# A gated-deltanet and MLP kernel on one core: half-chunk solves in one 64-row product, key loads on one queue, a new order list

## The chip, the cores and the metric

The kernel runs on one core of a Trainium2 chip. The metric is the device time of one execution in microseconds; the kernel before takes 277.19 us (median of three runs, 276.89 to 277.89). The profile is of one further execution, with a span of 275.1 us from the first to the last instruction. PE is TensorE, DVE is VectorE, ACT is ScalarE, POOL is GpSimd, and SP is SyncE, which here only issues DMA transfers.

## The reference

Two stages follow each other: a recurrence over 768 time steps for 4 batches of 8 heads with 48 features, and a two-layer MLP with a softplus between (3072 tokens, 384 to 2048 to 384).

```python
k_n = k / (norm(k) + 1e-6)
for t in range(S):                                   # S = 768
    readout = q[t] @ state                           # state: 48 x 48 per head
    y[t] = g[t] * readout
    v_old = state.T @ k_n[t]
    state = state + beta[t] * outer(k_n[t], v[t] - v_old)
x = y.transpose(0, 2, 1, 3).reshape(3072, 384)
out = softplus(x @ w_in) @ w_out
```

The readout at step t uses the state before step t. Inputs and outputs are float32; the kernel works in float16 with float32 accumulation.

## The kernel before

**Chunks.** The 768 steps are cut into 12 chunks of 64. Within a chunk the recurrence becomes a triangular system: with A the strictly lower part of the keys' products (scaled by beta and the norms), the corrected values u solve (1 + A) u = w, where w is v less what the state already holds for the keys. So each chunk needs the inverse of a 64 x 64 unit triangular block for each of 32 (batch, head) pairs. Two batches share the 128 partitions as 2 x 64 time steps; `HALF[r]` names those two ranges of 64, `QUAD[i]` the four ranges of 32, so `QUAD[2r]` is the first half of a chunk and `QUAD[2r + 1]` the second. The heads are split by m in two sets of eight, so most products come twice.

**Inverses.** Two neighbouring chunks are inverted together. The 32 x 32 diagonal blocks are inverted by column steps. For most pairs this is done as 16 x 16 blocks in 15 steps (`inverse`, L706; each step is one multiplication at L746 and one addition at L753), joined to 32 x 32 by the products `xmm` (L820) and `tmm` (L847). The steps run on VectorE for chunks 0 and 1, on GpSimd for the others. For chunks 8 and 9 (`LANES`) the 32 x 32 blocks are inverted directly in 31 steps on GpSimd (`wide_inverse`, L642; L679 and L685). Ahead of the steps stand the evicted key products, a transpose `ln` on VectorE (L713, L648) and the scales `bl` from beta and the norms (`lane_beta`, L394). After them come transposes on VectorE (L770, L779, L696) and casts on ScalarE (L800, L807, L701) to the tile `td`.

**Half blocks.** `halves` (L869) prepares, from the inverted diagonal blocks `td` and the keys' cross block, a tile `z`: its second-half rows are a copy of `td` made by an identity product (L879), its first-half rows the product of the cross block with `td` (L882).

**The chain of a chunk** (`chain`, L930): products of keys with the state, `ks` (L951); w on VectorE (L995, or L964 for chunk 0), after v was scaled by the norms at L973; `umm` (L1006), the diagonal blocks times w; a copy u1 to SBUF; `qs` (L951), queries with the state; `zu` (L1043), which adds the cross term to the second half; a copy u2; `smm` (L1076), the state's update, added on VectorE (L1093, state `s`); `ymm` (L1106), the outputs; the product with g (L1128); and a transpose into `xt`, by TensorE (L1147) for chunks 0 to 3 and 11, else by DMA.

**The MLP** (`dense`, L1178) takes the chunks in pairs, the first two and the last two singly: groups of up to six matmuls into `h` (L1194), the softplus on ScalarE (L1208), and groups of four matmuls into `o` (L1224), a copy and two stores. It has 96 groups of each of the two kinds.

**Loads.** k, q, v and g of a chunk come as two transfers of 192 KB each (`load`, L260). The rings of buffers are short: three for k, v and g, two for q. A load waits on its issuing engine until its buffer is free, and everything behind it waits too. Nearly all loads are issued by SyncE; `BY_ACT` (L121) names those that ScalarE issues. The weights are loaded by GpSimd in eight quarters, each held until a named load has landed.

**Order.** The program adds some 1137 items to a `Plan`, each with an engine, a cost, dependencies and buffers. A list written out at the end of the file, `_TABLE`, then says in which order they are issued: P112 is item 112 on TensorE, D on VectorE, A on ScalarE, G on GpSimd, S on SyncE. `follow` (L71) walks the list, hands out buffers and issues the instructions. It reads neither costs nor priorities: those serve whoever made the list. Each engine executes its items in the list's order, and an item that waits holds all that stand behind it on its engine.

Of the kernel before, what the change touches and what calls it, by code (L numbers as in the profile page):

```python
# [93 lines left out]
def kernel(  # L94
# [11 lines left out]
    nc = tc.nc  # L106
    B, H, S, D = q.shape
# [13 lines left out]
    BY_ACT = (("k", 0), ("k", 2))  # L121
# [31 lines left out]
    ident = pool.tile([P, P], F16, name="ident")  # L153
# [91 lines left out]
    HALF = [slice(0, 64), slice(64, 128)]  # L245
# [3 lines left out]
    def hd(ap):  # L249
        return ap[:, : H * D].rearrange("p (h d) -> p h d", h=H)  # L250
# [391 lines left out]
    def wide_inverse(cs, kk, kk_it, bl, bl_it, prio, prio2):  # L642
# [46 lines left out]
        for j in range(31):  # L689
            prev = add(  # L690
                "POOL", "step", 0.52 + 3.2e-3 * (31 - j) * (j + 1), lambda j=j: step(j),
                deps=[prev], bufs=[nn, tt, tmp], prio=prio,
            )
# [12 lines left out]
    def inverse(cs, kk, kk_it, bl, bl_it, on_dve, clear, prio, prio2, apart=0):  # L706
# [53 lines left out]
        for j in range(15):  # L760
            prev = add(
                en, "step", (0.42 if on_dve else 2 * fix) + 4 * per * (15 - j) * (j + 1), lambda j=j: step(j),
                deps=[prev], bufs=[nn, tt, tmp], prio=prio,
            )
# [165 lines left out]
    def chain(c, pr):  # L930
# [71 lines left out]
        def umm(m):  # L1002
            for pi in range(H):
                u = 16 * cl + 2 * pi + m
                for qd in range(4):
                    nc.tensor.matmul(  # L1006
                        hd(up[m].ap)[QUAD[qd], pi],
                        td.ap[QUAD[qd], u, :],
                        w1[m].ap[QUAD[qd], pi],
                        start=(pi == 0),  # L1010
                        stop=False,
                        skip_group_check=True,
                    )
# [3 lines left out]
                "PE", "umm", 0.22, lambda m=m: umm(m), deps=[a2[m], td_it],  # L1017
                bufs=[td, w1[m], up[m], u1[m]], prio=pr, mm=32, mode="3232",
# [21 lines left out]
        def zu(m):  # L1040
            for pi in range(H):
                for r in range(2):
                    nc.tensor.matmul(  # L1043
                        hd(up[m].ap)[QUAD[2 * r + 1], pi],
                        z.ap[QUAD[2 * r], 16 * cl + 2 * pi + m, :],
                        u1[m].ap[QUAD[2 * r], pi],
                        start=False,
                        stop=(pi == H - 1),
                        skip_group_check=True,
                    )  # L1050
# [4 lines left out]
                bufs=[z, u1[m], up[m], u2[m]], prio=pr, order=[c0], mm=16, mode="3232",  # L1055
# [246 lines left out]
S1 S0 A3 D111 P112 A2 D104 P105 G134 D135 A114 D107 A113 G132 S8 D133 A106 P115 P108 S6 D110 S9  # L1302
D118 S7 D109 A5 A4 S17 A136 A204 P205 D137 D138 A116 A117 D139 D140 D141 D142 D143 D144 D145 D146
D147 D148 D149 D150 D151 D152 D153 D154 D155 D156 P119 D157 D158 G97 A206 A207 P208 A197 G96 S10
S11 G227 G98 D159 P198 A199 A200 P201 A203 S18 A160 P162 A161 A190 S16 D125 D163 G103 A202 D169
P164 A165 S19 S20 D210 A209 D168 D228 S23 P166 D167 G99 P170 A172 D232 P174 A121 D120 P122 A189
D123 P171 D173 P175 P191 A177 G225 D176 D124 D226 A192 P126 D127 P183 S13 S12 D184 P181 D182 P178
A229 S39 S38 D230 P187 S22 A266 S21 D447 D128 D179 S14 S15 D211 A275 P276 S37 G267 P268 D269 D180
G100 A278 A188 P185 A186 P811 D231 S28 S29 A812 P212 A270 A214 P193 D277 P799 P279 D559 A194 P560
P813 D562 P195 G297 D281 D561 D213 P564 P129 D280 D298 A566 A196 P567 P569 A571 P563 D131 D130  # L1310
P577 D565 P568 S31 S30 D218 P219 S32 S33 D578 A814 D570 G102 P575 A299 A220 D221 P572 P222 D300
A800 D573 S47 P801 A802 D576 D574 S46 D224 P579 A580 G233 G234 S55 D223 P803 D271 S54 S36 S25 G235
G236 G237 A804 G238 G101 G239 G240 P581 G241 G242 G243 G244 D582 G245 G246 G247 G248 G249 P215
D216 G286 P287 P272 D273 P282 G250 G251 D252 D283 A289 P827 A288 D284 P805 A274 A828 S62 A254 A806
A346 P293 P809 D295 S24 P290 D291 G301 S45 S50 P256 S44 P829 A830 S60 P257 D253 A810 D294 D302
A258 S61 D217 D292 D285 D303 P837 S51 D296 D304 A368 D369 G607 P807 A808 P584 S63 P815 A255 G583
D586 D585 G357 G305 A838 P831 G306 G307 G308 P816 S27 P259 P817 P818 A832 P260 P839 A261 P262 P347
D349 A819 S49 A348 P264 D265 P835 P821 D263 S48 S35 G309 G310 S81 A836 G311 P588 D590 G312 G313
G314 P587 A589 A840 P591 P592 G315 G316 G317 S26 D652 P822 P593 P841 A595 P601 A370 D594 P599 P596
P823 D598 D597 P833 P608 P824 D602 A834 D600 D610 P612 P615 D371 G318 G319 A825 D609 A614 P603  # L1320
G320 G321 A604 S820 P617 G322 G323 P611 P605 D606 P843 A842 G342 A613 P616 A619 D618 P343 P620
P625 D324 P623 P844 A441 S34 A344 A326 D626 S80 S71 D624 P629 P627 P845 A338 S70 G417 A345 D628
P418 A419 D630 D622 P358 A420 A360 P865 A866 D359 G372 P328 D442 P855 A856 P361 D325 D363 S43 D362
P879 A880 P863 D621 P861 P329 P339 A327 D330 D340 P364 P332 A862 S85 S52 D365 S40 D373 D366 P885
G376 D367 D374 S41 A341 A864 A886 P859 A860 S84 P846 A847 S53 A439 P873 A874 D440 A496 P632 G631
S826 D633 P331 D634 P877 P869 A870 P353 D355 P350 P849 A333 D351 P334 A335 P636 P867 A868 S42 S69
A878 P850 P851 S90 P635 A637 D352 D354 D356 D375 P871 A872 G443 P639 P336 P640 D642 A638 P641 P857
A643 P644 D646 D645 A858 P883 A884 S78 S848 S59 P852 A853 P875 D409 P653 D654 P887 D655 S79 A337
P881 P410 D444 G377 G378 G379 G380 G381 G382 G383 G384 P656 P649 D412 D411 S68 A518 G428 P647 G385
D650 S56 D648 G386 G387 G388 G389 G390 P429 P657 P660 A876 A658 G391 A659 A882 G392 G393 P661 D445  # L1330
P662 P888 A664 P670 P889 P890 S76 D430 D431 D671 D519 A663 G394 S64 P668 S77 D669 P665 D666 A891
P421 P893 P894 P895 P896 S65 S651 D395 D422 A413 P414 D667 D423 A397 A416 A415 S854 P424 P399 P400
A897 D425 D396 A398 P435 S57 D436 A401 D426 S672 P917 D427 D437 P899 P900 P901 A918 P902 S892 A903
P432 D434 P941 A942 S91 D433 P905 P906 P915 A916 P919 A920 P674 P911 D438 P403 D446 A912 P402 P937
G520 D521 D673 D675 P907 A404 P939 A938 D676 S58 P405 D522 S898 A940 P908 P935 D523 P678 A936 P677
P927 S75 P925 G507 P508 A406 P681 A679 A680 S72 P683 A928 D509 A926 P929 P933 A510 D909 P682 A930
A684 D685 P407 P691 P689 D690 D692 A934 P913 P686 P497 D498 D687 D688 P921 G694 A914 D408 P931
S904 P943 S910 S67 A922 P695 G448 D697 P923 A492 P493 A932 P699 D696 P698 D499 S66 A924 D524 P944
P945 P946 A488 P489 A494 A495 P702 A700 P703 A701 S83 P704 A947 D490 S86 A706 G449 G450 G451 S693
S73 S948 P949 P712 G452 D705 G453 G454 G455 G456 G457 S82 P710 G458 G459 D713 G460 G461 G462 G463  # L1340
G464 G465 G466 G467 P950 P951 P952 G468 D711 A953 D491 P503 D504 D505 S714 P511 D513 D512 G469
G470 P955 G471 G472 G473 P956 P957 G474 G475 G476 G477 P958 G478 G479 G480 A959 P707 D708 D709
P500 D502 D501 P969 A970 S960 S89 P977 A978 P961 P514 P716 P971 A972 P989 D506 A990 P962 P979 A980
D515 P981 P991 A982 D516 D517 D525 S88 G481 A992 D482 P973 A974 P967 A968 P983 A984 A483 P963 P964
A965 S954 P985 A986 S87 D715 D718 P993 P484 A994 D717 P720 P719 P723 A485 D721 P987 D722 A988 P997
A998 P724 P486 S74 P725 P999 P975 D736 A727 D726 P728 D729 A976 G526 G527 G528 G529 G530 G531 G532
G533 G534 G535 G536 G537 G538 G539 P995 G540 D730 P733 D734 A996 G541 P731 G542 P737 G543 P1000
P1001 G544 G757 D732 D739 P1002 A1003 D738 P740 D742 S92 S93 S966 P741 P744 P1005 P1006 P1007
S1004 D546 A743 A487 P745 D747 P746 D748 P1008 A548 A1009 P752 P749 P754 P1011 P1012 D545 A547
P1013 P1014 D755 S735 D753 A1015 S756 P550 P549 A551 P1017 P1018 P1019 P1049 P1035 P552 A1050  # L1350
A1036 S1016 P553 P1027 A1028 P1023 A1024 P1020 S1010 D751 P1051 A1052 P1025 D750 P758 D760 D759
P1045 A1026 P1041 D554 A1046 A1042 P1031 A1032 P1039 A1040 P555 P761 P762 D764 P1043 A556 P765
P767 A763 P766 A1044 D1021 S1022 A769 P1033 A1034 P1037 A1038 S94 D768 P770 D771 D772 P1053 P1029
G778 A1030 P779 P775 S95 P773 D776 D780 P1047 P1055 P1056 D774 S777 A1054 P1057 D781 A1048 P1058
# [36 lines left out]
```

## Time and profile before

| What | Value |
|---|---|
| time, median of three | 277.19 us |
| span of the profiled run | 275.1 us, mean granted clock 0.969 |
| TensorE busy | 226.1 us |
| dense matmuls L1194 and L1224 | 77.2 and 71.3 us, 384 each |
| softplus on ScalarE, L1208 | 56.7 us, 96 |
| GpSimd 31 long steps, L679 and L685 | 16.7 and 17.1 us |
| GpSimd 60 short steps, L746 and L753 | 22.0 and 23.1 us |
| `umm`, L1006 | 9.7 us, 768 matmuls |
| `zu`, L1043 | 8.7 us, 384 matmuls |
| DMA moved | 29.07 MB, mean 106 GB/s |
| loads of k, q, v, g | median 4.7 to 6.0 us from issue to landing |

In the profile, busy time is the time in which an engine has an instruction in flight. Matmuls are pipelined, and a matmul that waits inside a group can count as busy, so a full row of TensorE doesn't mean that it works at its peak. The slices cut the span into 40 parts of 6.9 us, each digit being a share in tenths. Idle time of an engine is listed with what ended it. Item numbers of the order list don't appear in the profile: there an instruction is known by its line and its tiles.

### The profile page before, as it was taken

What the parts mean: (1) busy time and instruction counts of PE and PEld (TensorE: products, weight loads), DVE (VectorE), ACT (ScalarE), POOL (GpSimd) and SP (SyncE); (2) the same over time, 40 slices, a digit from 0 to 9 for tenths busy, and PEclk for the clock granted to TensorE, in tenths of its full rate; (3) what the DMA queues carried; (4) which work ended last, traced back from release to release, by engine and by line L of the source; (5) the groups of instructions that cost most, each with busy time, mean ns of one, the idle gap of its engine ahead of it and who ended that gap; (6) DMA issues with size and microseconds to landing.
All of it is one profiled execution on the core that took longest, in us unless ns stands there. A gap on an engine that the chain in (4) does not pass through costs nothing.

```text
span 275.1 us, 13296 instructions
## 1 busy us (share of the span) xinstructions
PE 226.1 (82%) x6030; PEld 150.5 (55%) x6030; DVE 165.7 (60%) x318; ACT 134.8 (49%) x230; POOL 141.1 (51%) x247
## 2 busy tenths in 40 slices
PE   0540357969898879999999999997599999999986
PEld 0430246757666555555665666553356655668754
DVE  6498589588996626896779956691757123412000
ACT  2241635433764357967447567154536356235620
POOL 8660023888917885287844788888887000000000
PEclk9999999995999979999999999999599999999999
DMA  8999999999998948455993146653312303400312
GB/s 109 144 174 193 173 164 156 181 175 150 142 160 140 135 75 169 84 104 97 151 150 61 33 90 122 116 115 59 64 27 62 76 17 63 84 14 20 71 46 61
DMA packets 113304, 29.07 MB, mean 106 GB/s; under 512 B 106464, under 2 KB 113248, under 8 KB 113248
## 3 DMA queue, kind: packets, MB, share of 16 engines
q1 hardware_dynamic: 105120, 24.19, 53.6%
q0 software_dynamic: 3968, 3.25, 7.6%
q10 hardware_dynamic: 4160, 0.79, 2.4%
q8 instruction: 47, 0.77, 1.2%
q14 instruction: 9, 0.07, 0.1%
HBM read 25.26 MB, written 4.72 MB: 109 GB/s over the span
## 4 chain that ended last, share of the span: by engine, by line
PE 39%; POOL 23%; DVE 11%; DMA 8%; issue 7%; SPq 6%; ACT 3%; DVEq 0%; POOLq 0%; ACTq 0%
PE o L1224 13%; PE h L1194 13%; SPq L268 6%; POOL t L685 6%; POOL tmp L679 6%; DMA qf<-in_q_dram 6%; POOL tt L753 4%; POOL tmp L746 4%; DVE kkm L599 3%; DMA gf<-in_g_dram 2%; PE d L1006 2%; PE d L1043 1%; DVE ln L713 1%; PE d L951 1%; PE d L882 1%
## 5 line engine op out<-in xcount | busy, mean ns | idle before, releaser
L1194 PE MATMUL h<-xt,w_in 128*128 128x512 f16 (+1 forms) x384 | 77.2, 338 | 0.9 <-ACT xt L236 0.6
L1208 ACT ACTIVATE ga<-h 128x512 f16<-128x512 f32 x96 | 56.7, 598 | 40.6 <-PE h L1194 39.3
L1224 PE MATMUL o<-w_out,ga 128*128 128x384 f16 x384 | 71.3, 329 | 1.3 <-DVE osb L238 0.7
L1224 PEld LDWEIGHTS <-ga 128*128 128x128 f16 x384 | 35.8, 98 | 24.4 <-issue 1.9
L1194 PEld LDWEIGHTS <-w_in 128*128 128x128 f16 x384 | 35.6, 101 | 22.6 <-issue 3.3
L433 PE MATMUL d<-ident,kn 128*128 128x128 f16 x96 | 9.4, 258 | 19.6 <-ACT kn L236 10.0
L753 POOL TENSOR_TENSOR tt<-tt,tmp 128x30 f32<-128x30 f32 (+7 forms) x60 | 23.1, 385 | 4.7
L746 POOL TENSOR_TENSOR tmp<-nn,tt 128x30 f32<-128x30 f32 (+7 forms) x60 | 22.0, 367 | 4.5
L236 ACT ACTIVATE u<-d 128x384 f16<-128x384 f32 x28 | 13.3, 492 | 21.8 <-PE d L1043 10.9
L236 ACT ACTIVATE kqx<-d 128x512 f16<-128x512 f16 x27 | 15.0, 593 | 16.2 <-PE d L433 13.4
L599 DVE TENSOR_TENSOR kkm<-d,both 128x512 f16<-128x512 f32 x32 | 20.5, 676 | 2.1 <-PE d L589 2.1
L236 ACT ACTIVATE osb<-o 128x384 f32<-128x384 f32 x19 | 9.3, 489 | 25.2 <-PE o L1224 23.1
L995 DVE TENSOR_TENSOR w<-vf,d 128x384 f16<-128x384 f32 x22 | 11.4, 548 | 15.3 <-ACT ga L1208 11.0
L330 POOL TENSOR_TENSOR ksq<-kf 128x768 f32<-128x768 f32 x6 | 9.1, 1522 | 22.3 <-DMA gf<-in_g_dram 18.5
L433 PEld LDWEIGHTS <-kn 128*128 128x128 f16 x96 | 7.5, 116 | 22.6 <-ACT kn L236 11.8
L238 DVE CAST u<-d 128x384 f16<-128x384 f32 x20 | 10.8, 553 | 14.1 <-PE d L1006 9.4
L363 POOL TENSOR_TENSOR nv<-nv,half_c 128x32 f32<-128x32 f32 x3 | 16.3, 5445 | 5.4 <-DVE nv L340 5.4
L685 POOL TENSOR_TENSOR t<-t,tmp 128x31 f32<-128x31 f32 (+15 forms) x31 | 17.1, 551 | 2.4
L679 POOL TENSOR_TENSOR tmp<-n,t 128x31 f32<-128x31 f32 (+15 forms) x31 | 16.7, 539 | 2.4
L1128 DVE TENSOR_TENSOR yg<-d,gf 128x384 f16<-128x384 f32 x24 | 12.4, 550 | 6.3 <-PE d L1106 6.3
L238 DVE COPY osb<-o 128x384 f32<-128x384 f32 x5 | 2.8, 553 | 20.8 <-PE o L1224 20.8
L1093 DVE TENSOR_TENSOR s<-d,s 128x384 f16<-128x384 f32 x20 | 10.4, 551 | 7.8 <-PE d L1076 7.8
(112 smaller groups left out, 376.8 us busy)
## 6 DMA issues: line engine op xcount, KB each, us to landing
qf<-in_q_dram SPq DMA_DIRECT2D x24, 192.0 KB, 5.6
vf<-in_v_dram SPq DMA_DIRECT2D x24, 192.0 KB, 5.6
gf<-in_g_dram SPq DMA_DIRECT2D x24, 192.0 KB, 4.7
out_dram<-osb SPq DMA_DIRECT2D x48, 96.0 KB, 3.1
kf<-in_k_dram SPq DMA_DIRECT2D x20, 192.0 KB, 5.6
w_in<-in_moe_w_in_dram POOLq DMA_DIRECT2D x4, 384.0 KB, 10.8
w_out<-in_moe_w_out_dram POOLq DMA_DIRECT2D x4, 384.0 KB, 6.5
kf<-in_k_dram ACTq DMA_DIRECT2D x4, 192.0 KB, 6.0
```

What stands on the lines that cost most here:

```text
L236: nc.scalar.activation(o, x, AF.Copy, scale=float(sign))
L268: (nc.scalar if (name, c) in BY_ACT else nc.sync).dma_start(out=b.ap[64 * b2 : 64 * b2 + 64].rearrange("t p h d -> t (p h) d"), in_=x[2 * ...
L363: nc.gpsimd.tensor_tensor(x, x, half_c[:, sl], ALU.pow)
L433: nc.tensor.transpose(f16ps(tp.ap)[:, P * i : P * i + P], n.ap.rearrange("t p h d -> t (p h d)")[:, P * i : P * i + P], ident,)
L599: nc.vector.tensor_tensor(kkm.ap[:, u0 : u0 + 7 : 2], gb[m].ap.rearrange("p (n t) -> p n t", t=2 * C), both[:, None, :].broadcast_to([P, N ...
L679: nc.gpsimd.tensor_tensor(t, nn.ap[:, j + 1 :, j : j + 1].broadcast_to([P, n, w]), tt.ap[:, j : j + 1, :w].broadcast_to([P, n, w]), ALU.mult,)
L685: nc.gpsimd.tensor_tensor(tt.ap[:, j + 1 :, :w], tt.ap[:, j + 1 :, :w], t, ALU.add)
L746: eng.tensor_tensor(t, nn.ap[:, :, j + 1 :, j : j + 1].broadcast_to([P, 2, n, w]), tt.ap[:, :, j : j + 1, 16 : 16 + w].broadcast_to([P, 2, ...
L753: eng.tensor_tensor(rows, rows, t, ALU.add)
L1194: nc.tensor.matmul(hp.ap[:, n * b : n * b + n], w_in[:, j, f * P : (f + 1) * P], xt.ap[:, t0 // P : (t0 + n) // P, j], start=(j == 0), sto ...
L1208: lambda hp=hp, o=gb: nc.scalar.activation(o.ap, hp.ap, AF.Softplus),
L1224: nc.tensor.matmul(op.ap[:, :DM], b.ap[:, col + c0 : col + c0 + 128], w_out[:, f, :], start=(f == 0), stop=(f == NF - 1),)
```

## The change

Four things change.

First, the solve of a chunk's second half. Before, `umm` multiplied all four quarters with their diagonal blocks, and `zu` added the cross term to the second half by accumulation in PSUM. Now `umm` computes the first halves only, and puts w itself, by an identity product, where the second halves will be. The copy u1 then holds the first half's solution and the second half's w, and `zu` forms the second half's solution in one product over 64 rows, with `z` as the weights: its first-half rows are the cross block's, its second-half rows the copy of `td`. No accumulation is left in it. It is meant to spare matmuls: 18 in place of 32 in each `umm`.

Second, `BY_ACT` is empty: the keys of chunks 0 and 2 are issued by SyncE, like all others.

Third, the costs that the list's maker assumes for the steps on GpSimd are raised, and the cost of `umm` by a little.

Fourth, the order list is new as a whole. It is meant to suit the changed costs. Its beginning is shown before and after; the rest differs in the same manner.

```diff
-    BY_ACT = (("k", 0), ("k", 2))
+    BY_ACT = ()
...
-                "POOL", "step", 0.52 + 3.2e-3 * (31 - j) * (j + 1), lambda j=j: step(j),
+                "POOL", "step", 0.67 + 3.2e-3 * (31 - j) * (j + 1), lambda j=j: step(j),
...
-                en, "step", (0.42 if on_dve else 2 * fix) + 4 * per * (15 - j) * (j + 1), lambda j=j: step(j),
+                en, "step", (0.42 if on_dve else 0.6) + 4 * per * (15 - j) * (j + 1), lambda j=j: step(j),
...
         def umm(m):
+            for r in range(2):
+                f = QUAD[2 * r + 1]
+                nc.tensor.matmul(hd(up[m].ap)[f], ident[f, f], w1[m].ap[f])
             for pi in range(H):
                 u = 16 * cl + 2 * pi + m
-                for qd in range(4):
-                    nc.tensor.matmul(
-                        hd(up[m].ap)[QUAD[qd], pi],
-                        td.ap[QUAD[qd], u, :],
-                        w1[m].ap[QUAD[qd], pi],
-                        start=(pi == 0),
-                        stop=False,
-                        skip_group_check=True,
-                    )
+                for r in range(2):
+                    f = QUAD[2 * r]
+                    nc.tensor.matmul(hd(up[m].ap)[f, pi], td.ap[f, u, :], w1[m].ap[f, pi])
...
                     nc.tensor.matmul(
                         hd(up[m].ap)[QUAD[2 * r + 1], pi],
-                        z.ap[QUAD[2 * r], 16 * cl + 2 * pi + m, :],
-                        u1[m].ap[QUAD[2 * r], pi],
-                        start=False,
-                        stop=(pi == H - 1),
-                        skip_group_check=True,
+                        z.ap[HALF[r], 16 * cl + 2 * pi + m, :],
+                        u1[m].ap[HALF[r], pi],
                     )
...
-S1 S0 A3 D111 P112 A2 D104 P105 G134 D135 A114 D107 A113 G132 S8 D133 A106 P115 P108 S6 D110 S9
+S2 S3 A104 P105 A132 D133 S0 D107 S1 A111 P112 A106 G134 D135 D113 P108 A114 P115 S4 S5 A136 D110
...
```

In the list, S0 and S1 are the two halves of the load of k1, S2 and S3 of k0, S4 and S5 of k2, S6 and S7 of k3; A2 to A5 before are k0 and k2 on ScalarE. Where the two lists differ matters by stage, and three differences are spoken of below. The squares of the keys of chunks 0, 2 and 3 (L330 on GpSimd, L332 on ScalarE) move from GpSimd to ScalarE, and with them the cast of the keys of chunk 4. The list before puts 19 dense groups on TensorE ahead of the last `umm` of chunk 2, the new one 13. And between the last product of chunk 9's keys and the first use of the 31-step inverse the list before puts 47 dense and 31 small groups, the new one 52 and 33.

## Prediction

> **What bounds the kernel now.** I read the page first: busy times, then the forty slices.
>
> ```profile
> PE 226.1 (82%) x6030; PEld 150.5 (55%) x6030; DVE 165.7 (60%) x318; ACT 134.8 (49%) x230; POOL 141.1 (51%) x247
> ...
> PE   0540357969898879999999999997599999999986
> ...
> PEclk9999999995999979999999999999599999999999
> DMA  8999999999998948455993146653312303400312
> ```
>
> One slice is 6.9 us. PE (TensorE) is nearly idle for six slices, then nearly full to the end, except about slices 28 and 29 (190 us), where the clock falls too. The DMA engines are full for twelve slices, the time of the thin PE. So there are two stages: up to some 90 us the recurrence waits for loads and for VectorE, ScalarE and GpSimd; after that PE has work without end. PE is the bound there, and a wait costs time only where the order has no matmul to put before it.
>
> The stage table gives 6.49, 5.31, 15.53, 18.27 and 15.61 us of PE in the first five stretches of 20 us: 61 of 100. From 100 to 260 us it gives 19.35, 19.61, 19.34, 19.99, 15.34, 19.38, 19.96 and 20.00. The loss is in the start and in one hole.
>
> The timeline of each engine shows what makes the start slow (start, duration, engine, line, what; in brackets the idle time before it and what ended it):
>
> ```profile
> 26.52 0.84 ACT L236 ACTIVATE kn<-kf 128x768 f16<-128x768 f32 x1 [8.47 <-DMA kf<-in_k_dram]
> ```
>
> ```profile
> 37.30 1.46 POOL L330 TENSOR_TENSOR ksq<-kf 128x768 f32<-128x768 f32 x1 [18.49 <-DMA gf<-in_g_dram]
> ...
> 45.72 0.82 POOL L238 CAST kn<-kf 128x768 f16<-128x768 f32 x1 [6.96 <-PE d L1076]
> ...
> 51.12 0.24 POOL L726 COPY tt<-bl 128x32 f32<-128x32 f32 x1 [1.05 <-DVE bl L394]
> ```
>
> ScalarE stands 8.47 us for the keys of chunk 2, whose load ScalarE issued itself at 12 us behind other work. GpSimd stands 18.49 and 6.96 us for inputs of its squares and casts, so the inverse of chunks 2 and 3 starts there at 51.12 us. It ends at 68.2, and the first products with it (L1006 of chunk 2) start at 87.22 us.
>
> The hole at 190 us:
>
> ```profile
> 152.10 1.62 POOL L667 TENSOR_TENSOR n<-ln,bl 128x256 f32<-128x256 f16 x2 [4.48 <-DVE ln L648]
> ```
>
> ```profile
> 192.39 1.25 DVE L696 STREAM_TRANSPOSE t<-t 128x1024 f32<-128x1024 f32 x1 [5.55 <-POOL t L685]
> ```
>
> ```profile
> 195.68 0.61 PE L879 MATMUL d<-td,ident 32*32 32x512 f16 x2 [4.59 <-ACT td L701]
> ...
> 197.68 2.74 PE L1194 MATMUL h<-xt,w_in 128*128 128x512 f16 x6
> ```
>
> The 31-step inverse of chunks 8 and 9 holds GpSimd from 152.1 to 192.4 us. PE runs out of work 4.59 us before its result comes through VectorE and ScalarE, and then six dense matmuls take 2.74 us; six such take 1.40 elsewhere on the chain of waits.
>
> **What the Trainium skill says.** "TensorE: Matmul & The Clock Gate", Part 1, has PE's clock fall to half after an idle window of about 3.4 us. The trace agrees: after the wait of 4.59 us one slice has clock 5, and the stretch of 180 to 200 us a mean of 0.84. The same page, Part 3, "The mechanism", lets a weight load overlap matmuls in flight only in another row group. That bears on the new identity products; the trace is consistent (next part). "TensorEngine Tiling (Array Packing)", "Key Properties", has a change of tiling mode drain PE; no row here isolates that. "DMA: Bandwidth & Descriptors", "Issuing engines are not separate DMA queues", says that a second issuing engine saves only issue time, as all share 16 DMA engines. The trace agrees: those are full until 80 us, whoever issues.
>
> **The change part by part.** *Inverse products.* Before, a chunk has 64 matmuls L1006 on four row groups (64 take about 0.59 us, 9.2 ns each) and 32 of L1043 on two row groups (about 0.32 us a half). After, each of the 24 halves has 16 of L1006's kind, on two row groups, and two identity products of 384 columns.
>
> ```profile
> 84.20 0.39 PE L879 MATMUL d<-td,ident 32*32 32x512 f16 x2
> 84.21 0.58 PE L882 MATMUL d<-td,kkm 32*32 32x32 f16 x32
> ```
>
> This is the same construct: two identity products and 32 small ones take 0.53 us to the next group's start, and 32 small ones at 10 ns are 0.32, so the pair costs about 0.21, one pass of 512 columns: the two run side by side, and what follows on their row groups waits. In the new product what follows is on the other two row groups. Sixteen at 15 ns (L1043's spacing on two row groups) are 0.24; the identity pair of 384 columns is 0.16 (L1224's spacing), hidden at best, in series at worst: 0.24 to 0.40 against 0.295 per half, so -1.3 to +2.5 us over 24. I take the middle, +0.6. L1043's 16 matmuls keep count and columns; 64 rows instead of 32 cost nothing I can see. Its new mode can add a drain, at most 0.1 us (the usual lag where shapes change) x 24 = 2.4. I take 0, since its neighbours mostly have other shapes already. The chain of steps per chunk is as long as before.
>
> *Planner's costs.* Nothing reads them at run time: zero. But 31 steps and their gaps took 38.6 us (153.8 to 192.4). The old cost sums to 0.52 x 31 + 0.0032 x 5456 = 33.6, the new to 38.2; fifteen short steps took about 13.2 without the foreign work between them, against 12.1 old and 13.3 new. The new list was thus made with true lengths, the old one thought the hole of 4.59 us covered.
>
> *Loads.* ScalarE loses four issues (2.9 us of its queue); it idled beside them. Loads then come in SP's order alone: k0, k1, k2, k3, v0 first half, q0, v1. In the trace loads land about 1.2 us apart when no weights run (eleven from 36.35 to 49.62), the first at 5.0. So load n lands at about 3 + 1.2 n, plus 1.4 to 2.6 us for each quarter of weights ahead of it (eight hold their queue 7.6% of 275 us, 2.6 each; five went in 12.9 us among five loads, 1.4). Then k2 is there at 10 us, not 26.
>
> *New order, start.* The squares of chunks 2 and 3 and the cast of k4 leave GpSimd. Ahead of its first inverse stand one square, the scaling of v1 (waits for load 14, 20 us; the weight issues queue behind it, wanted only after 50), and the cast of q4 (load 19, 30 to 34 us). It also needs VectorE's L394, which now follows chunk 0's products; these start about 31.5 instead of 37.0, as VectorE's inverse starts at 14 instead of 17.6. I put this inverse at 39 instead of 51 us. v2 is load 40: with six to eight weights 59 to 72 us, against 73.85. So chunk 2's L1006 should start near 76, 11.2 us earlier. Against that, the new list has 13 dense groups before it, not 19, and two small groups fewer: 6 x 0.655 + about 1.0 = 5.0 us of PE work that moves behind it. Net: -6.2.
>
> *New order, hole.* Between the last gram of chunk 9 and the first consumer of the long inverse the list has 52 dense groups instead of 47, and 33 small groups instead of 31: 47.6 us of PE work against 43.2 by measured group lengths. The path beside it is unchanged (L648 150.08 to L1006 196.5 = 46.4). So 4.4 of the 4.59 us is covered, and the cold clock after it (half speed from 195.7 to 200.5, 2.4 us) does not come: -6.8.
>
> Sum: 277.2 + 0.6 - 6.2 - 6.8 = 264.8; I say 265.
>
> **The rivals.** *The start gives nothing net*: chunk 2 comes only the 5.0 us earlier that the moved work costs. For it: DMA is full whoever issues, and ScalarE now casts q5 (load 30) ahead of a copy in chunk 1's chain. Then 277.2 + 0.6 - 6.8 = 271. *Slower*: chunk 2 comes no earlier, the moved 5.0 us is simply late, and since that delays the grams of chunks 8 and 9 no less than the filler, the hole stays: 277.2 + 0.6 + 5.0 = 282.8. For it: k7 is now load 58 (before 46), about 93 us or later, and VectorE's reduction of its square stands between the two halves of chunk 3's state update, so chunk 4 waits behind it. Against it: that update was at 103 us before. *Even*: one of the two gains turns into a new hole of its size, 277.
>
> **How the numbers follow.** Both gains 0.62 (265), hole alone 0.15 (271), even 0.07 (277), slower 0.16 (283). The first spreads by the unknown prices: the products from -1.3 to +4.9, v2 over 59 to 72 us and other small waits, so 259 to 270. The range 259 to 277 leaves out the slower case and the edge of the first. Faster by over 0.5%: 0.77; same 0.07; slower 0.16.
>
> **What would show it.** Right: ScalarE's wait for k2 gone; the first L726 on GpSimd near 39 us; chunk 2's first L1006 near 76; L1006's group and the identity pair together 0.24 to 0.40 us a half; no clock 5 near 190 us, and PE's wait for L701 under 1 us. Wrong: chunk 2 at 85 us or later; a wait of VectorE for k7's square over 3 us; a new PE wait over 3.4 us with a cold slice after it.

## The result and the profile after

The changed kernel takes 268.32 us (median of four runs, 266.39 to 270.14) against 277.04 beside it: ratio 0.968, 95% interval 0.961 to 0.975. Timed once more, it took 268.24 us, ratio 0.966 (0.962 to 0.970). The forecast was 265.0. Some executions of a kernel are slower than its others; the ratios leave these out and the medians don't, so the two can differ by up to 0.8%, and four of the profiles below (the order alone, the hole filled, and the half-block shifts of the changed kernel and of the kernel before) are of such an execution.

The page of the changed kernel, busy times and slices (one slice is now 6.6 us):

```profile
PE 223.5 (84%) x5694; PEld 148.8 (56%) x5694; DVE 159.2 (60%) x311; ACT 138.8 (52%) x238; POOL 138.4 (52%) x246
...
PE   0551357599879889999999999999999999999996
...
PEclk9999999999997999999999999999999999999999
DMA  7999999979989992295971589680913202250212
```

TensorE is busy for 64.0 us in the first five stretches of 20 us, where it was 61.2. The dip at slices 28 and 29 is gone, and so is its low clock. The table by stretches has the same from 180 to 200 us (columns: length, then busy time and instructions of PE, PEld, DVE, ACT, POOL, the clock, DMA share, GB/s), where the kernel before had 15.34 us of PE at clock 0.84:

```profile
180.00:200.00 20.00, 19.48 (x525) 11.51 (x524) 9.41 (x17) 11.73 (x20) 17.34 (x41) 1.00 0.36 72
```

The lines that answer to the start, from the timelines of ScalarE and GpSimd:

```profile
12.31 0.83 ACT L236 ACTIVATE kn<-kf 128x768 f16<-128x768 f32 x1
```

```profile
44.42 0.24 POOL L726 COPY tt<-bl 128x32 f32<-128x32 f32 x1 [6.71 <-DVE bl L394]
...
73.23 1.48 POOL L973 TENSOR_TENSOR vf<-vf,nv 128x768 f32<-128x768 f32 x1 [0.24 <-DMA vf<-in_v_dram]
```

The cast of chunk 2's keys comes at 12.31 us without a wait, before it was 26.52. GpSimd's inverse of chunks 2 and 3 starts at 44.42 instead of 51.12 us, after 6.71 us of waiting for VectorE. The second line is new here: the values of chunk 2 are scaled as soon as they land, at 73.1 us.

And the hole, on GpSimd and on TensorE:

```profile
140.66 1.62 POOL L667 TENSOR_TENSOR n<-ln,bl 128x256 f32<-128x256 f16 x2 [2.60 <-DVE ln L648]
```

```profile
183.53 1.46 PE L1188 MATMUL h<-xt,w_in 128*128 128x512 f16 x6
184.92 0.34 PE L1005 MATMUL d<-w,ident 32*32 32x384 f16 x2
184.96 0.29 PE L1010 MATMUL d<-w,td 32*32 32x48 f16 x10
...
185.31 0.39 PE L879 MATMUL d<-td,ident 32*32 32x512 f16 x2
```

Chunk 8's product with the long inverse now follows a dense group directly. (In the changed kernel `umm` is L1005 and L1010, `zu` L1040, the dense groups L1188 and L1218.)

Landmarks of the two profiled executions, in us; `umm` means the chunk's first:

| | before | after | difference |
|---|---|---|---|
| `umm` of chunk 0 | 37.0 | 33.4 | -3.6 |
| `umm` of chunk 2 | 87.2 | 81.1 | -6.1 |
| `umm` of chunk 6 | 157.1 | 150.1 | -7.0 |
| long inverse starts on GpSimd | 152.1 | 140.7 | -11.4 |
| `umm` of chunk 8 | 196.3 | 184.9 | -11.4 |
| end | 275.1 | 264.7 | -10.4 |

So 6 to 7 us come in the start, 4.4 between chunks 6 and 8, and 1 us is given back behind.

### The profile page after: what moved, and what is told of

Same layout as the page of the kernel before. It is cut to its first block, busy times and chain, and to the rows that moved or that the text cites. A ratio compares the mean times of both kernels' runs of the same rounds, so it can differ in the third digit from the quotient of the medians.

```text
span 264.7 us, 12630 instructions
## 1 busy us (share of the span) xinstructions
PE 223.5 (84%) x5694; PEld 148.8 (56%) x5694; DVE 159.2 (60%) x311; ACT 138.8 (52%) x238; POOL 138.4 (52%) x246
## 4 chain that ended last, share of the span: by engine, by line
PE 59%; DMA 4%; DVE 3%; issue 1%; ACT 1%; SPq 0%; DVEq 0%; ACTq 0%
PE o L1218 21%; PE h L1188 20%; PE d L951 3%; PE d L1100 2%; DMA xt<-yg 2%; PE d L433 2%; PE d L1040 2%; DMA out_dram<-osb 1%; PE d L882 1%; PE d L589 1%; PE d L847 1%; PE d L1010 1%; PE d L1070 1%; PE d L820 1%; PE h L909 1%; DVE yg L1122 1%
## 5 line engine op out<-in xcount | busy, mean ns | idle before, releaser
L1188 PE MATMUL h<-xt,w_in 128*128 128x512 f16 (+1 forms) x384 | 75.2, 333 | 1.8 <-DVE xt L238 0.6
L1218 PE MATMUL o<-w_out,ga 128*128 128x384 f16 x384 | 70.8, 327 | 1.1 <-ACT osb L236 0.6
L1218 PEld LDWEIGHTS <-ga 128*128 128x128 f16 x384 | 35.5, 98 | 24.8 <-issue 1.9
L1188 PEld LDWEIGHTS <-w_in 128*128 128x128 f16 x384 | 35.4, 100 | 21.8 <-issue 2.8
L753 POOL TENSOR_TENSOR tt<-tt,tmp 128x30 f32<-128x30 f32 (+7 forms) x60 | 22.5, 374 | 4.7
L599 DVE TENSOR_TENSOR kkm<-d,both 128x512 f16<-128x512 f32 x32 | 20.7, 681 | 3.0 <-PE d L589 3.0
L236 ACT ACTIVATE osb<-o 128x384 f32<-128x384 f32 x19 | 9.3, 489 | 24.3 <-PE o L1218 15.9
L236 ACT ACTIVATE kqx<-d 128x512 f16<-128x512 f16 x28 | 16.2, 598 | 9.3 <-PE d L433 6.6
L973 POOL TENSOR_TENSOR vf<-vf,nv 128x768 f32<-128x768 f32 x9 | 13.2, 1475 | 11.5 <-DMA vf<-in_v_dram 11.5
L679 POOL TENSOR_TENSOR tmp<-n,t 128x31 f32<-128x31 f32 (+15 forms) x31 | 17.4, 562 | 2.4
L238 DVE CAST u<-d 128x384 f16<-128x384 f32 x19 | 10.4, 554 | 13.4 <-PE d L1040 10.1
L995 DVE TENSOR_TENSOR w<-vf,d 128x384 f16<-128x384 f32 x22 | 11.4, 546 | 8.7 <-PE d L951 4.2
L1087 DVE TENSOR_TENSOR s<-d,s 128x384 f16<-128x384 f32 x20 | 10.3, 551 | 8.7 <-PE d L1070 8.6
```

Source lines behind the costliest of these rows:

```text
L236: nc.scalar.activation(o, x, AF.Copy, scale=float(sign))
L599: nc.vector.tensor_tensor(kkm.ap[:, u0 : u0 + 7 : 2], gb[m].ap.rearrange("p (n t) -> p n t", t=2 * C), both[:, None, :].broadcast_to([P, N ...
L679: nc.gpsimd.tensor_tensor(t, nn.ap[:, j + 1 :, j : j + 1].broadcast_to([P, n, w]), tt.ap[:, j : j + 1, :w].broadcast_to([P, n, w]), ALU.mult,)
L753: eng.tensor_tensor(rows, rows, t, ALU.add)
L1188: nc.tensor.matmul(hp.ap[:, n * b : n * b + n], w_in[:, j, f * P : (f + 1) * P], xt.ap[:, t0 // P : (t0 + n) // P, j], start=(j == 0), sto ...
L1218: nc.tensor.matmul(op.ap[:, :DM], b.ap[:, col + c0 : col + c0 + 128], w_out[:, f, :], start=(f == 0), stop=(f == NF - 1),)
```

## First experiments: one part at a time

All kernels below were timed beside the kernel before (277.3 to 277.7 us in these groups).

**Products alone**: the kernel before, with the new `umm` and `zu` only.

> The kernel before with the new products alone (umm with the identity pair, zu over 64 rows), old list, old key queues. Theory (the traces: a chunk's two halves of umm take 0.52 us instead of 0.59, of zu 0.51 instead of 0.58): about 0.14 us x 12 = 1.7 us less of TensorE, of which a little drowns in the hole at 190 us, so 275 to 276. Rival (the prediction's own price of +0.6 us): 277 to 278.

Measured 279.37 us, ratio 1.0063 (1.0034 to 1.0092): slower, against both theories.

**Order alone**: the changed kernel with the old products, so the new list and the one key queue.

```diff
         def umm(m):
-            for r in range(2):
-                f = QUAD[2 * r + 1]
-                nc.tensor.matmul(hd(up[m].ap)[f], ident[f, f], w1[m].ap[f])
             for pi in range(H):
                 u = 16 * cl + 2 * pi + m
-                for r in range(2):
-                    f = QUAD[2 * r]
-                    nc.tensor.matmul(hd(up[m].ap)[f, pi], td.ap[f, u, :], w1[m].ap[f, pi])
+                for qd in range(4):
+                    nc.tensor.matmul(
+                        hd(up[m].ap)[QUAD[qd], pi], td.ap[QUAD[qd], u, :], w1[m].ap[QUAD[qd], pi],
...
```

> The kernel after with the old umm and zu: new list and one key queue alone. Theory: the order brings nearly all, so 268.3 + 1.7 = 270. Rival (the products are worth nothing, or cost 0.6 us): 267.5 to 268.3. Second rival (the products bring most): above 273.

Measured 281.0 us, ratio 1.0097 (1.0063 to 1.0132): slower by 1%, where 270 was expected.

**Hole filled**: the kernel before, with five dense groups moved ahead of the first consumer of the long inverse (P985 to P1000 in its list), nothing else.

> The kernel before, but in its list four groups of L1194 and two of L1224 that stood behind the first use of the 31-step inverse stand ahead of it (3.9 us of TensorE work), with their softplus copies. Nothing else is moved. Theory (the hole of 4.59 us and the cold clock after it were lost time): TensorE's wait there falls to about 0.7 us, no slice with clock 5 near 190 us, 277.0 - 3.9 - 2.4 = 270.7. Rival (the work that fills the hole is missed later, where the chain of chunks 8 to 11 then has nothing beside it): 275 to 277.

Measured 277.98 us, ratio 0.997 (0.994 to 1.000): next to nothing, and by the ratio what the rival said (275 to 277). But the rival's reason, that the moved work is missed later, doesn't show: from 220 to 260 us TensorE is busy for 39.96 of 40 us. The time goes right behind the hole, in a stop in the middle of a group and a low clock after it (timeline, row of the clock, stretch from 200 to 220 us):

```profile
203.96 0.27 PE L1043 MATMUL d<-u,z 32*32 32x48 f16 x5 [2.91 <-issue]
```

```profile
PEclk9999999955999977999999999999968999999997
```

```profile
200.00:220.00 20.00, 16.05 (x529) 10.98 (x529) 10.42 (x20) 6.60 (x9) 11.57 (x24) 0.83 0.27 55
```

What such a stop is comes below.

**Keys back on ScalarE**: the changed kernel with the old issue of k0 and k2.

```diff
-    BY_ACT = ()
+    BY_ACT = (("k", 0), ("k", 2))
...
-S2 S3 A104 P105 A132 D133 S0 D107 S1 A111 P112 A106 G134 D135 D113 P108 A114 P115 S4 S5 A136 D110
+A2 A3 A104 P105 A132 D133 S0 D107 S1 A111 P112 A106 G134 D135 D113 P108 A114 P115 A4 A5 A136 D110
```

> The kernel after with the keys of chunks 0 and 2 issued by ScalarE again, at the places of their items in the new list. Theory (k2 then is issued at about 12 us and lands near 18 to 20; the new list has the cast of k2 ahead of the key copies that the first inverse waits for, so the first chain starts some 6 us later): 271 to 274, TensorE's first L820 at 35 instead of 29 us. Rival (the start is bound by DMA whoever issues): 268, L820 at 29 to 31.

Measured 277.23 us, ratio 0.9996 (0.997 to 1.002): the whole gain is lost, more than the 271 to 274 us expected. Its timelines of ScalarE and VectorE show how:

```profile
22.70 0.84 ACT L236 ACTIVATE kn<-kf 128x768 f16<-128x768 f32 x1 [6.77 <-DMA kf<-in_k_dram]
23.45 1.55 ACT L236 ACTIVATE kkm<-d 128x512 f16<-128x512 f32 x3
```

```profile
25.04 1.92 DVE L713 STREAM_TRANSPOSE ln<-kkm 128x1024 f16<-128x1024 f16 x1 [7.56 <-ACT kkm L236]
```

The first copies of key products (`kkm`) stand behind the cast of chunk 2's keys in ScalarE's new order, and VectorE's first transpose L713 waits for them 7.56 us. In the changed kernel the same transpose starts at 14.64 us. The 10.4 us between go through to the end, as 9 to 11 us: `umm` of chunk 0 comes at 42.7 instead of 33.4, of chunk 2 at 90.2 instead of 81.1, and the span is 275.8 instead of 264.7.

So the parts don't add up: +1.0% for the order with the key queue, +0.6% for the products, -3.2% for both. Something that no part contains must differ between these kernels.

## What the profiles of the parts had in common

In the timeline of TensorE of the order alone there is a stop in the middle of a group, with nothing to wait for ("issue"):

```profile
70.20 0.36 PE L589 MATMUL d<-kqx 48*64 48x128 f16 x12
74.57 0.32 PE L589 MATMUL d<-kqx 48*64 48x128 f16 x4 [4.01 <-issue]
```

Twelve of 16 matmuls run, then nothing for 4.01 us. VectorE's next step, L599, waits for the last four:

```profile
75.00 0.69 DVE L599 TENSOR_TENSOR kkm<-d,both 128x512 f16<-128x512 f32 x1 [3.94 <-PE d L589]
```

The Trainium skill, "Runtime: NRT & Kernel Launch", section "Instruction fetch mechanics", has an engine's instructions arrive in blocks of 16 KiB, which are 256 instructions, by a DMA queue of its own while the block before executes. The page has such a queue; here of the kernel before and of the changed one (packets, MB, share of 16 engines):

```profile
q8 instruction: 47, 0.77, 1.2%
```

```profile
q8 instruction: 44, 0.72, 1.2%
```

That is 16.4 KB a packet, and 256 x 47 = 12,032 against 12,066 recorded instructions of TensorE (matmuls and weight loads) before, 256 x 44 = 11,264 against 11,396 after. So the page's block size agrees. The same section calls the cost of a block's border "mostly hidden"; that doesn't agree here. The trace holds each packet's time. The packet that goes with the stop of 4.01 us ran from 71.49 to 73.00 us: it started after TensorE had stopped, and TensorE went on 1.58 us after it had landed. In all 14 profiles (the changed kernel has two) there are 107 stops of 0.3 us or more inside a group without a recorded wait, and every one ends 1.2 to 1.9 us after one of these packets landed. By chance about 12% would (47 windows of 0.7 us in 275). The count of instructions says the same more sharply. Numbering TensorE's recorded instructions from the first, each of the 107 stops comes right behind number 256 k + 192 or 193, and k is then the number of these packets that have landed when it ends. The stops lie at the borders of the blocks and nowhere else.

Theory A, then: the stops are TensorE out of instructions, and where the program is cut into blocks decides what is hit and what that costs. Theory B: the gain is made by order, products and data alone, and the stops only fill time in which TensorE would have waited anyway. A shift of the cuts tells them apart.

## Second experiments: moving the cuts

Tiny matmuls go ahead of TensorE's first work. They run from 1.69 to 3.56 us (64 of them), when TensorE has nothing to do until the first keys at 6.9. Each is two instructions; nothing else changes.

```diff
-    def fill(prio):
+    def fill(prio, count=40):
...
-            for _ in range(40):
+            for _ in range(count):
...
+    fill(-500, 64)
     plan.follow(_TABLE)
...
 _TABLE = """
+P1137
```

**The changed kernel again, unaltered.**

> The changed kernel, unaltered, timed beside the shifted kernels of this group so that all are compared on one chip. Both theories: 268 us, ratio near 0.968, with a narrower interval than before. If it comes out above 271, the gain of the first timing was partly luck and the sizes of all earlier comparisons have to be read anew.

Measured 268.24 us, as above.

**The changed kernel, shifted by half a block** (64 matmuls).

> The changed kernel with 64 tiny matmuls (128 TensorE instructions) put ahead of TensorE's first work, where it waits for the first keys until 6.9 us anyway; nothing else of the order, the data or the other engines is touched. What moves is where TensorE's program is cut into its blocks of 256 instructions: by half a block. Theory A (each stall in the middle of a group, with nothing to wait for in the profile, is TensorE out of instructions; the cut decides which group is hit, and a few us of the time hang on it): the stalls inside groups move to other groups, each still ending 1.2 to 1.8 us after an instruction block landed, and the time moves by 2 us or more, to 270-277, since the changed kernel's cuts happen to be good ones. Theory B (the gain is made by the order and the products and their data alone): the time stays within 1 us of the unaltered changed kernel, 267-269.

Measured 276.4 us, ratio 0.989 (0.986 to 0.993): by the ratios 2.4% more than without the shift (0.989 / 0.966). The stops at 42 and 52 us of the changed kernel are gone, and others come, such as this one:

```profile
68.97 0.25 PE L589 MATMUL d<-kqx 48*64 48x128 f16 x4
72.15 0.54 PE L589 MATMUL d<-kqx 48*64 48x128 f16 x12 [2.93 <-issue]
```

The granted clock goes along. It is 0.962 to 0.981 in all executions of this kernel, against 0.987 to 1.000 in those of the unaltered one beside it. In its profile:

```profile
PEclk9999999999689796899999999999999999999999
```

The stretches at half clock from 71.5 and from 105.6 us, 6.8 us each, begin while TensorE stands in its two longest stops.

**The kernel before, shifted by half a block.**

> The kernel before with the same 64 tiny matmuls ahead of TensorE's first work. Theory A: the 2.4 us stall at 95 us and the 1 us stalls at 58 and 82 us move or shrink, others come; the time moves by more than 1 us either way, between 272 and 280. Theory B: 277 within 1 us.

Measured 282.65 us, ratio 1.016 (1.011 to 1.020): moved by more than 1 us, and beyond the range that theory A gave.

**The order alone, shifted by half a block.**

> The new list and the key queue with the old products (the order alone, 281.0 us) and the same 64 tiny matmuls ahead of TensorE's first work. Its profile had 17.8 us of stalls inside groups, 4.0 us of them at 70 us ahead of the second chunk's work. Theory A: the cut was a bad one here; half a block further the stalls inside groups sum to 5-12 us and the time falls to 270-277. Theory B: the order without the new products is slow of itself, 280-282.

Measured 280.62 us, ratio 1.008 (1.004 to 1.012): a miss for theory A's forecast, and inside theory B's. The stops sum to 15.9 us here too, against 15.6 without the shift (stops of 0.3 us or more; the expectation's 17.8 was another count), so this run can't tell bad cuts at both places from an order that is slow with the old products. The run with more instructions below goes at that.

**The changed kernel, shifted by a whole block** (128 matmuls), the control: the cuts fall where they fell, but the tiny matmuls are doubled.

> The changed kernel with 128 tiny matmuls (256 TensorE instructions, one whole block) ahead of TensorE's first work; from the run with 64 they take 1.87 us per 64, so they end near 5.5 us, ahead of the first keys at 6.9. The cuts between blocks fall where they fell without them, one block further on. Theory A (TensorE out of instructions; the cut decides): the stalls inside groups are those of the unaltered kernel, near 42, 52 and 57 us, 4-6 us in sum, and the time is 268-270. Rival (the tiny matmuls themselves cost the 8 us that the shift by 64 cost, by the clock or by one block more to fetch): 276 or more.

Measured 268.16 us, ratio 0.969 (0.963 to 0.974). The stop near 50 us, first of the unaltered changed kernel, then of the control:

```profile
50.12 0.58 PE L589 MATMUL d<-kqx 48*64 48x128 f16 x13 [0.16 <-DVE kqx L238]
52.32 0.75 PE L589 MATMUL d<-kqx 48*64 48x128 f16 x19 [1.62 <-issue]
```

```profile
50.81 0.58 PE L589 MATMUL d<-kqx 48*64 48x128 f16 x13 [0.16 <-DVE kqx L238]
52.76 0.74 PE L589 MATMUL d<-kqx 48*64 48x128 f16 x19 [1.36 <-issue]
```

Both stop after the same 13th matmul of the same group. So the tiny matmuls themselves cost nothing that can be seen, and it is the place of the cut that costs the 2.4%. That is theory A.

**The changed kernel, shifted by three quarters of a block** (96 matmuls).

> The changed kernel with 96 tiny matmuls (192 instructions, three quarters of a block) ahead of TensorE's first work. Theory A: a third place for the cuts; somewhere between 266 and 278, with the sum of the stalls inside groups going along with the time. If the changed kernel's own cuts are only ordinary, this one is near 268 too; if they are lucky ones, it is 272-277.

Measured 270.31 us, ratio 0.973 (0.966 to 0.980). The unaltered cuts are good ones, but not uniquely so.

**As many instructions as the old products**: the changed kernel with 14 tiny matmuls into unused columns ahead of each half of `umm`.

```diff
         def umm(m):
+            for i in range(14):
+                f = QUAD[i % 4]
+                nc.tensor.matmul(up[m].ap[f, 384:400], ident[f, f], ident[f, f][:, :16])
             for r in range(2):
```

> The changed kernel with 14 tiny matmuls into unused columns ahead of each half of the block-and-inverse product, so that it issues as many TensorE instructions at the same places as with the old products (672 more in all); results and the products themselves as in the changed kernel. Direct cost at 29 ns each, from the first work of the shifted runs: 24 halves x 14 x 29 ns = 9.8 us if all lie on the path, less where TensorE waits or the four quarters run beside each other. Theory A (the old products' loss under the new list, 281.0 us, is their number of instructions): 276-282. Rival (the old products lose by their structure, a longer dependent chain through the four quarter products): 268-273.

Measured 279.4 us, ratio 1.010 (1.005 to 1.014), the same as the order alone with its old products. By TensorE's start times the 24 halves of `umm` take 8.7 us with the tiny matmuls and 5.9 without, so 2.8 us are direct cost; the medians differ by 11.2. The rest goes with the cuts, and these are those of the order alone: its stop of 4.01 us came after 12 of 16 of L589, and here one comes at the same place, though it is shorter:

```profile
72.20 0.36 PE L589 MATMUL d<-kqx 48*64 48x128 f16 x12
73.77 0.25 PE L589 MATMUL d<-kqx 48*64 48x128 f16 x4 [1.21 <-issue]
```

So the number of instructions, and where it puts the cuts, is enough to lose what the old products lose under the new list. That their structure costs nothing besides is not shown, as the tiny matmuls have 2.8 us of their own.

**Key queue alone in the kernel before**: k0 and k2 to SyncE at their places of the old list; TensorE's program is the same.

> The kernel before, with only the first keys' loads of chunks 0 and 2 given to the one queue of the other keys, at their places of the old list; TensorE's, VectorE's and GpSimd's instructions are the same, so the cuts between instruction blocks don't move. It tells what the key queue is worth without the new list. Prediction's reading (ScalarE's 7.1 us wait for the third chunk's keys goes, but the order behind it is unchanged): 274-277. Rival (the key queue alone makes most of the gain, as its return to ScalarE lost all of it in the changed kernel): 268-271. Third reading (the keys of chunk 0 now come behind others and the first chunk starts late): 278-282.

Measured 276.49 us, ratio 0.9996 (0.996 to 1.003): nothing that can be told from zero. `umm` of chunk 2 comes at 86.8 instead of 87.2.

All profiles side by side. "Ahead" is the number of TensorE instructions put in front; stops are those inside groups of 0.3 us or more, of one execution each, and not all lie on the path that sets the end. "Half clock" is the time at half the clock in the same execution, without the stretch that begins when TensorE has ended.

| kernel | ahead | blocks | stops, sum in us | half clock, us | median us | ratio |
|---|---|---|---|---|---|---|
| before | 0 | 47 | 6, 5.7 | 17.0 | 277.0 to 277.7 | 1 |
| before, keys on one queue | 0 | 47 | 5, 6.0 | 20.4 | 276.49 | 0.9996 |
| before, hole filled | 0 | 47 | 9, 10.5 | 27.3 | 277.98 | 0.997 |
| before, new products | 0 | 44 | 8, 10.3 | 17.1 | 279.37 | 1.006 |
| before, shifted | 128 | 47 | 12, 16.9 | 30.7 | 282.65 | 1.016 |
| after, both timings | 0 | 44 | 5, 4.0 and 4, 3.8 | 3.4 and 0 | 268.3 | 0.966 to 0.968 |
| after, keys on ScalarE | 0 | 44 | 5, 3.6 | 3.4 | 277.23 | 0.9996 |
| after, whole block | 256 | 45 | 7, 6.6 | 3.4 | 268.16 | 0.969 |
| after, three quarters | 192 | 45 | 7, 8.7 | 6.8 | 270.31 | 0.973 |
| after, half | 128 | 45 | 8, 9.6 | 17.0 | 276.4 | 0.989 |
| after, more instructions | 0 | 47 | 9, 10.7 | 10.2 | 279.4 | 1.010 |
| after, old products | 0 | 47 | 11, 15.6 | 20.4 | 281.0 | 1.010 |
| after, old products, shifted | 128 | 47 | 11, 15.9 | 20.4 | 280.62 | 1.008 |

Of the changed kernel's own variants with one list and one key queue, time rises with the sum of stops, from 4 us at 268 to 16 us at 281, though not in proportion: 8.7 and 9.6 us of stops go with 270 and 276 us, and there the half clock differs, 6.8 against 17.0 us. Of the 35 stretches at half clock in all profiles, 23 begin between 0.5 us before a stop and 2 us behind its end, and these windows are about 10% of the time (both are commoner before 110 us). So a stop probably costs more than its length; no run changed the clock alone.

The change itself, before against after at the same number of instructions ahead, is worth 3.2 to 3.4% without a shift and 2.6% with half a block (0.989 / 1.016).

## Why the prediction was right, and where not

The time, 268.3, lies 3.3 us above the forecast, inside the range and on the side of the likeliest case. The total held because the kernels before and after happen to have about the same stops, 5.7 and 4.0 us. Had the cut fallen half a block later in the changed kernel alone, the ratio would have been 0.989 in place of 0.966 to 0.968, about 274 us. That the forecast came so close is in this part luck. The prediction's list of risks did not contain this term at all.

- **Products, +0.6 forecast.** By start times the 24 halves of `umm` took 7.1 us before and 5.9 after, 0.25 us a half; `zu` took 6.0 and 5.9. So -1.2 us: the lower end of the range given, with the identity pair hidden and no drain for the new mode. The mis-sized part is what the step left out, the 670 fewer instructions. Alone in the old list they came with worse stops and +0.6%; in the new list the old products cost 12.7 us (281.0 - 268.3). The product's own time is the small part of its effect.
- **Loads.** k2 at 10 us was right (its cast ran at 12.31 without a wait). That this wait mattered was right only together with the order: taken away alone it gave nothing, and put back under the new list it took 9 us. The prediction followed it to GpSimd's inverse of chunks 2 and 3. The run with keys on ScalarE shows another path, through `kkm` to VectorE's inverse of chunks 0 and 1.
- **Start, -6.2 forecast.** Near in size, wrong in its two terms, and in part made by the cuts. GpSimd's inverse was put at 39 us and came at 44.42, as L394 stood behind L713 and state copies on VectorE. The values of chunk 2 were put at 59 to 72 us and landed at 73.1, nearly where they did before (73.85); w followed at 76.2 and 79.1. So chunk 2 came 6.1 instead of 11.2 us earlier. That is little more than the 5.0 us of dense work moved behind it, which was to be given back; but at chunk 6 the lead was still 7.0. Between the first `umm` of chunk 2 and that of chunk 6 the changed kernel does 57 dense groups, the kernel before 53. At 0.655 us each that is 2.6 us more work, yet it takes 0.9 us less. In this stretch the kernel before has three stops inside groups, 3.2 us in sum, and the changed one has none. So the moved work was largely paid, and the missing stops hid it. This is worked out from one profile of each and not tried by a run of its own. Ahead of the first `umm` of chunk 2 the changed kernel has seven dense groups fewer (six ahead of the last); three of them, 2.0 us, are still owed at chunk 6.
- **Hole, -6.8 forecast.** The lead grows from 7.0 to 11.4 us between chunks 6 and 8, the 4.4 that was forecast, and the low clock is gone. From `umm` of chunk 8 to the end it took 79.8 us against 78.7, with 73.5 instead of 71.0 us of work, an estimate from measured group lengths. The time beyond that work fell from 7.7 to 6.3, so 1.4 us are there where the forecast had 2.4 for the cold clock. Filled alone, the hole gave 0.3% and came with stops of 10.5 us instead of 5.7. The one of 2.91 us right behind the hole ends in 6.8 us at half clock, from 203.6 us, as long a stretch as that of the kernel before from 193.7. That these ate the gain is argued, as this kernel wasn't shifted.
- **Clock.** The prediction, by the Trainium skill ("TensorE: Matmul & The Clock Gate", Part 1), looked for a cold clock only behind an idle time of about 3.4 us, so only at the hole. The traces differ, and they decide. The row of the clock that it shows has two more dips, in slices 10 and 15. They are half clock for 6.8 us from 60.6 and 3.4 us from 98.1, behind stops of 1.08 and 2.38 us; in the 3.4 us before, TensorE was busy for 1.6 and 1.0 us. In the changed kernel only 3.4 us from 79.8 are left, so more of the gain is clock than the forecast allowed for.
- **Rivals.** None was the case as a whole. The first came near in its premise, as chunk 2 came 6.1 us earlier for 5.0 us of moved work; its sum, with the hole, was 271. The slower one, k7 as load 58, did not bite: k7 landed at 96.7 us, and VectorE's waits for squares (L340 for GpSimd's L330) between 90 and 115 us were 0.4 us at most, against the 3 us named as a sign.

In the kernel before, several stops are on the path itself, this one the longest. It is a piece of the chain of waits that sets the end (start, duration, what):

```profile
95.46 2.38 issue
```

It lies inside `umm` of chunk 3. The change moved this cut too, so some of the gain can be luck of the cut. With two cuts tried of the kernel before and three of the changed one, how much is not settled; a gain of 2.6 to 3.4% stands at the two that can be compared.

## What to carry to other kernels

A timeline with stops "issue" in the middle of a group of small matmuls says that an engine ran out of instructions; look at the packets of the instruction queue before looking for a dependency. In a program with thousands of tiny matmuls, any edit that changes their number or order also moves the cuts, by which this kernel moved up to 2.4%, so a single-part experiment needs a control: the same edit at another shift, or an edit that leaves that engine's program alone. Fewer instructions for the same work can be worth more than the time of the work itself (12.7 against 1.2 us under the new list), or cost something (0.6% under the old).

## What was not expected of the hardware

- TensorE stopped for up to 4.01 us inside a group and went on 1.2 to 1.9 us after a packet of 16 KB of instructions had landed, in all 107 cases, and all 107 lie at a border of 256 instructions.
- A block is asked for late: the packet starts in the median 1.2 us after TensorE has passed the border before it (544 of 626 packets start after that border). So TensorE seems to have about one block ahead, and small matmuls, some 9 to 15 ns apart, can use it up before the next is there.
- The packets themselves took only 0.9 to 1.8 us. In the longest case the packet started 0.9 us after the stop had begun (70.56 by the group's end, 71.49). What makes a packet start later still is open: 75 of the 107 stops lie before 110 us, where the DMA engines are fullest, and by profile the median start is 1.4 to 2.1 us behind the border from 30 to 110 us and 0.7 to 1.1 us later on. But the stop of 2.91 us with the hole filled lies at 201 us, and there the DMA share from 198 to 205 us is 0.45. No run changed the DMA traffic alone.
- A whole block of tiny matmuls, 3.58 us of TensorE work, cost nothing that can be seen in the start's idle time and kept the stop near 50 us at the same matmul.
- The clock fell to half without 3.4 us of idle time: in the run shifted by a whole block from 88.6 us on, behind a stop of 0.88 us, with TensorE busy for 1.25 of the 3.4 us before.
